# More weight units converted during attention, tail work queued behind the evacuations, and two operands of x kept in float32

## The chip, the cores and the metric

The kernel runs on one core of a Trainium2 chip. The metric is the device time of one execution in microseconds, as the median of several. TensorE (PE in the profile) multiplies matrices into PSUM banks, VectorE (DVE), ScalarE (ACT) and GpSimd (POOL) work elementwise, and SyncE (SP) issues the DMAs. Each engine runs its own instructions in the order in which the program holds them.

## The reference

Attention with normalised queries and keys, and then two feed-forward blocks. The weights of both blocks come in float64.

```python
q_n, k_n = rmsnorm(q, g_q), rmsnorm(k, g_k)                # (4, 12, 448, 64)
attn = softmax(q_n @ k_n.T / 8)
x = (attn @ v).transpose(0, 2, 1, 3).reshape(1792, 768)
x = ((x @ w1) * (x @ w2) @ w3) @ w_out                     # 768 -> 1024 -> 1024 -> 768
h = x @ w_in                                               # 768 -> 2048
out = (h * clip(h + 3, 0, 6) / 6) @ w_out2                 # 2048 -> 768
```

## The kernel before, in words

Every float32 operand of a large product is split into a high and a low part (`t[:, 0]` by ACT, `t[:, 1]` as the difference, by DVE or POOL: `halves`), and a product is three matmuls. A float64 weight is turned into float32 on the chip by `convert`: two ACT instructions (L142, L143) and two DVE instructions (L145, L148).

The attention of 48 head pairs runs in steps of 112 x 448 scores (`attention`). In each step `fill` lets a filler go on: `products`, which makes w3 @ w_out first and then, batch by batch, `layer1` (x @ w1 and x @ w2, evacuated from PSUM by L366, L369 and L371) and `layer2` (with the folded w3 @ w_out, evacuated by L411 and stored to `x2d`). Their operand tiles `ws` are loaded again for each batch, three units ahead. `fill` also lets `early` go on, which converts weight units of the last block ahead of time, half a unit at a time: load into `raw`, convert, store as float32 to `wfd`. A unit is 128 x 768; `units2` lists the 32 units (16 of w_in, 16 of w_out2) in their order of use, and the last `NE` are converted in `early`. The others are `fresh`: they are loaded into `wr` and converted whole, into `wf`, by `units` and `spend`.

After the attention a loop (L1052 and on; the tail from here) runs the rest of `products`: the end of layer2 of the third batch, then layer1 and layer2 of the last one. Beside it go the fresh units and, from the end of the last layer1 on, the preparation of x for the first pair of batches (`xprep`), and of the first weights (`prep_to`).

The last block runs for two pairs of batches, p = 0 and 1. x @ w_in is made by a Strassen scheme with seven products (`ORDER`, P1 to P7) of nine matmuls each on 384-wide halves. Two PSUM banks, sA and sB, take them in turn: a product that adds to a bank, or starts it anew, waits until the bank's earlier content was copied (`L1123 u<-sA`, `u<-sB`) or added (L1131). The operands of x are 11, 21, T1, T2, T3 (from `xprep`), 22 and T4 (from `xrest`, which loads 22 again and makes T4 as the difference of the split parts of 21 and T2, by L976 to L978). Behind the Strassen products of p = 0 stands the M stage: 324 matmuls (items "M", layer4) on the second batch, whose operands `g` are split by `gsplit` (L1085, L1086), and beside which x of p = 1 is prepared by `xprep` and `xrest`.

A scheduler fixes the order on each engine when the program is built; `tc.issue_after(i)` makes what is written in its block stand behind instruction i on i's engine, and adds no wait for it.

Of the kernel before, what the change touches and what calls it, by code (L numbers as in the profile page):

```python
# [27 lines left out]
P = 128  # L28
# [17 lines left out]
NE = 18  # L46
# [5 lines left out]
def fused_kernel(ctx: ExitStack, tc: tile.TileContext, nat, qT, kT, vin, gq, gk,  # L52
# [103 lines left out]
    def products():  # L156
        yield from wprime()
        for b in range(B):
            yield from layer1(b)
            if b == 0:  # L160
                L["early"] = early()
            if b == B - 1:
                for _ in L["early"]:
                    pass
                L["xm"].__exit__(None, None, None)
                L["half"] = True
            yield from layer2(b)
# [136 lines left out]
    L = {}  # L304
# [3 lines left out]
    def open_l1():  # L308
# [14 lines left out]
        def item(u):  # L323
# [19 lines left out]
            else:  # L343
                src = w12d[r // 2, 1 - r % 2] if r < 2 * M1 else wpd[r - 2 * M1].rearrange("p k c -> p (k c)")
                dma(t.bitcast(F32).rearrange("p t c -> p (t c)"), src)
# [16 lines left out]
    def layer1(b):  # L362
        pool = L["pool"]

        def evac_b(ps, bs):
            nc.scalar.activation(bs, ps[:, :S], AF.Copy)  # L366

        def evac_a(m, ps, bs):
            nc.vector.tensor_mul(bs, ps[:, :S], bs)  # L369
            d = pool.tile([P, 2, S], F32R, tag="abh", bufs=M1, name="abh")  # L370
            nc.scalar.activation(d[:, 0, :], bs, AF.Copy)  # L371
            nc.vector.tensor_sub(d[:, 1, :], bs, d[:, 0, :])
            L["abh"][m] = d
# [32 lines left out]
    def layer2(b):  # L406
        pool = L["pool"]

        def evac(n, ps):
            st = pool.tile([P, S], F32, tag="bs", bufs=2, name="bs")  # L410
            nc.scalar.activation(st, ps[:, :S], AF.Copy)  # L411
            L["last"] = dma(x2d[b, n], st)

        for n in range(KD):
            ps = bank("f")
            for a in range(M1):
# [19 lines left out]
    def fill(us, aux):  # L436
# [7 lines left out]
        state["early"] = min(state["early"] + 0.7, 1.4)  # L444
# [435 lines left out]
    def units():  # L880
        n = 0
        for v, (kind, q) in enumerate(uses):
# [3 lines left out]
            if v in fresh:  # L886
                r = wr.pop(v)
# [5 lines left out]
                n += 1  # L893
                load_raw(n + 1)
# [52 lines left out]
    def xprep(p):  # L947

        b1, b2 = PAIRS[p]
        for k in range(KD // 2):  # L950
            x = {}
            for z, b, n in (("11", b1, k), ("21", b1, k + 3), ("12", b2, k), ("22", b2, k + 3)):
                x[z] = utile()
                dma(x[z], x2d[b, n])
# [3 lines left out]
            for z, src in (("11", x["11"]), ("21", x["21"]), ("T2", t2), ("T1", t1)):  # L958
                xo[z, k] = halves(xtile(z, k), src)
                yield 1.2  # L960
            nc.vector.tensor_sub(x["12"], x["22"], x["12"])
# [3 lines left out]
    def xrest(p):  # L965
        x = []
        for k in range(KD // 2):
            x.append(utile())
            dma(x[k], x2d[PAIRS[p][1], k + 3])
        yield 0.0  # L970
        for k in range(KD // 2):
            xo["22", k] = halves(xtile("22", k), x[k])
            yield 1.2
        for k in range(KD // 2):
            d = utile()
            nc.vector.tensor_sub(d, xo["21", k][:, 0, :], xo["T2", k][:, 0, :])  # L976
            nc.vector.tensor_sub(x[k], xo["21", k][:, 1, :], xo["T2", k][:, 1, :])
            nc.vector.tensor_add(d, d, x[k])  # L978
            xo["T4", k] = halves(xtile("T4", k), d)
            yield 1.8  # L980
# [62 lines left out]
    load_raw(1)  # L1043
# [8 lines left out]
    while not state["done"] or any(k >= now[0] for k in tasks):  # L1052
# [3 lines left out]
        if now[0] % 2 and "half" not in L:  # L1056
            spend(1.5)
        if "half" in L:
            if xg is None:
                xo["cm"] = tc.tile_pool(name="xl", bufs=1, side="left", **RW)  # L1060
                xo["pool", True] = d1.enter_context(xo["cm"])
                xg = xprep(0)
            for _ in range(2):
                if next(xg, None) is None:
                    prep_to(ready[0] + 1 if ready[0] < AHEAD2 else 0)
# [15 lines left out]
    G, g = {}, {}  # L1081

    def gsplit(p, b, q, src):
        t = rp.tile([P, 2, S], F32R, tag="g", bufs=4, name="g")
        nc.scalar.activation(t[:, 0, :], src, AF.Copy)  # L1085
        nc.vector.tensor_sub(t[:, 1, :], src, t[:, 0, :])  # L1086
# [73 lines left out]
    next(xg)  # L1160
    for i, it in enumerate(items):
# [6 lines left out]
        next(xg, None)  # L1168
# [58 lines left out]
```

## Time and profile before

| | us |
|---|---|
| median of the runs (3) | 1203.75 |
| lowest, highest | 1199.5, 1210.93 |
| the profiled execution | 1209.22 |
| its span, first to last instruction | 1207.4 |
| TensorE busy in it | 1144.1 (95%) |

TensorE's end times are modelled, so that 25 us of work without a gap show as 25 us busy; the number of its instructions in a stretch tells more. A row of a timeline has the start and the duration, and in brackets how long the engine sat idle before, and on what.

### The profile page before, as it was taken

The numbers are of one execution on the slowest core, as the hardware profiler recorded it, in microseconds if no ns is written. First come the engines' busy times: TensorE is split into PE (matmuls) and PEld (weight loads), VectorE is DVE, ScalarE is ACT, GpSimd is POOL, SyncE is SP. The second block draws the span as 40 slices with busy tenths as digits, with TensorE's granted clock in tenths as the row PEclk, the third lists the DMA queues.
The fourth block names the chain that finished last, engine by engine and source line by source line (L and its number), as shares of the span: only waits on it lengthen the run. The fifth ranks groups of instructions, "written<-read, shape, count | busy, mean of one in ns | idle before, by whom it ended". The sixth has DMA issues, their size and how long they took to land.

```text
span 1207.4 us, 17322 instructions
## 1 busy us (share of the span) xinstructions
PE 1144.1 (95%) x5596; PEld 977.9 (81%) x5596; DVE 844.8 (70%) x1775; ACT 762.0 (63%) x1589; POOL 352.7 (29%) x297
## 2 busy tenths in 40 slices
PE   3689899999999999999998999899999799999998
PEld 1345577788789998889998999699999699999997
DVE  6969887899788889887765456655547765555542
ACT  5869877888787787777754355455556455555542
POOL 1123312555333124222022013322224832223221
PEclk9799999899899999999999999899999999999999
DMA  8888755488999888887689887422236242222301
GB/s 270 281 288 288 255 156 161 156 265 267 330 338 316 286 289 295 283 284 256 226 302 405 319 305 284 162 89 66 84 90 226 89 150 80 71 87 74 125 31 46
DMA packets 88890, 252.71 MB, mean 209 GB/s; under 512 B 11232, under 2 KB 35040, under 8 KB 88800
## 3 DMA queue, kind: packets, MB, share of 16 engines
q1 hardware_dynamic: 88800, 251.61, 62.5%
q8 instruction: 44, 0.72, 0.2%
q14 instruction: 46, 0.38, 0.1%
HBM read 208.93 MB, written 42.64 MB: 208 GB/s over the span
## 4 chain that ended last, share of the span: by engine, by line
PE 74%; DVE 9%; DMA 7%; issue 4%; ACT 3%; POOL 2%; SPq 1%; ACTq 0%; DVEq 0%; POOLq 0%
PE bank L390 12%; PE sB L1111 8%; PE sA L1111 8%; PE bank L395 6%; PE acc L86 5%; PE acc L87 5%; PE acc L88 5%; PE bank L645 4%; PE bank L251 3%; PE bank L86 3%; PE bank L87 2%; PE bank L88 2%; PE bank L619 2%; PE bank L620 2%; PE bank L698 2%
## 5 line engine op out<-in xcount | busy, mean ns | idle before, releaser
L390 PE MATMUL bank<-xhl,ws 128*128 128x448 f32 x768 | 181.9, 370 | 3.3 <-ACT bs L366 3.1
L944 POOL TENSOR_TENSOR wt<-wf,wt 128x384 fp32r<-128x384 f32 x90 | 105.2, 1172 | 216.5 <-ACT wt L942 210.9
L390 PEld LDWEIGHTS bank<-xhl,ws 128*128 128x128 f32 x768 | 145.1, 190 | 17.3 <-ACT bs L366 3.4
L638 ACT ACTIVATE PP<-PP,mx 112x448 f32<-112x448 f32 x192 | 127.2, 663 | 41.1 <-DVE mx L633 39.1
L626 DVE CUSTOM_DVE_ANT_0 PP<-bank,rb,rq 112x448 f32<-112x448 f32 x192 | 128.7, 675 | 24.4 <-PE bank L620 14.7
L87 PE MATMUL acc<-g,wt 128*128 128x448 f32 x384 | 141.6, 369 | 3.5 <-DVE g L1086 3.5
L88 PE MATMUL acc<-g,wt 128*128 128x448 f32 x384 | 136.7, 370 | 4.7 <-POOL wt L944 3.5
L86 PE MATMUL acc<-g,wt 128*128 128x448 f32 x384 | 127.8, 369 | 0.0
L942 ACT ACTIVATE wt<-wf 128x384 fp32r<-128x384 f32 x176 | 89.8, 519 | 59.9 <-PE acc L88 36.1
L1111 PE MATMUL sA<-xo,wt 128*128 128x448 f32 x504 | 113.8, 368 | 3.4 <-ACT xo L942 2.5
L1111 PE MATMUL sB<-xo,wt 128*128 128x448 f32 x504 | 114.2, 371 | 1.3 <-ACT u L1123 1.2
L251 PE MATMUL bank<-woh,w 128*128 128x384 f32 x256 | 100.2, 518 | 10.9 <-DVE wst L244 7.2
L654 ACT ACTIVATE xh<-bank 128x448 fp32r<-128x448 f32 (+1 forms) x156 | 82.9, 539 | 35.8 <-PE bank L645 33.2
L1111 PEld LDWEIGHTS sA<-xo,wt 128*128 128x128 f32 x504 | 95.0, 189 | 12.8 <-ACT xo L942 3.3
L1111 PEld LDWEIGHTS sB<-xo,wt 128*128 128x128 f32 x504 | 95.7, 190 | 10.5 <-ACT u L1123 1.5
L645 PEld LDWEIGHTS bank<-ident,PP 112*128 112x128 f32 x672 | 79.2, 142 | 28.8 <-issue 10.8
L619 PE MATMUL bank<-K,Q 128*112 128x448 f32 x192 | 81.2, 424 | 21.6 <-ACT K L598 11.2
L645 PE MATMUL bank<-ident,PP 112*128 112x112 f32 x672 | 94.4, 262 | 3.7 <-DVE xl L664 3.1
L395 PE MATMUL bank<-xhl,ws 128*128 128x448 f32 x384 | 96.0, 368 | 0.0
L664 DVE TENSOR_TENSOR xl<-bank,xh 128x448 fp32r<-128x448 f32 x142 | 87.0, 616 | 8.7 <-ACT xh L654 7.6
L944 DVE TENSOR_TENSOR wt<-wf,wt 128x384 fp32r<-128x384 f32 x86 | 53.5, 623 | 52.1 <-ACT wt L942 49.3
L145 DVE SCALAR_TENSOR_TENSOR raw<-raw 128x384 int32<-128x384 int32 (+1 forms) x100 | 66.5, 667 | 28.8 <-ACT raw L143 27.8
(131 smaller groups left out, 2429.8 us busy)
## 6 DMA issues: line engine op xcount, KB each, us to landing
ws<-w12d SPq DMA_DIRECT2D x48, 768.0 KB
wf<-wfd SPq DMA_DIRECT2D x82, 384.0 KB
ws<-wpd SPq DMA_DIRECT2D x32, 768.0 KB
raw<-in_wo_dram SPq DMA_DIRECT2D x36, 384.0 KB
raw<-in_w_dram SPq DMA_DIRECT2D x32, 384.0 KB
w12d<-ws SPq DMA_DIRECT2D x16, 768.0 KB
qr<-in_qT_dram SPq DMA_DIRECT2D x24, 448.0 KB
kr<-in_kT_dram SPq DMA_DIRECT2D x24, 448.0 KB
```

Source lines behind the costliest of these rows:

```text
L86: nc.tensor.matmul(ps, lh, rh, start=first, stop=False)
L87: nc.tensor.matmul(ps, lh, rl, start=False, stop=False)
L88: return nc.tensor.matmul(ps, ll, rh, start=False, stop=last)
L251: nc.tensor.matmul(ps[:, :NH], W["w3"][a, c // 4][:, cs], W["woh"][c, n], start=c == 0, stop=c == M1 - 1)
L390: nc.tensor.matmul(ps[:, :S], w[:, 0, ks], x[:, y, :], start=k == 0 and y == 0, stop=False)
L395: nc.tensor.matmul(ps[:, :S], w[:, 1, ks], L["xhl"][i][:, 0, :], start=False, stop=k == KD - 1)
L619: nc.tensor.matmul(ps[:CP, :S], qs, k1[:, j, :], start=True, stop=False)
L626: anchors[8 * i + s].append(nc.vector.tensor_tensor_reduce(out=T["PP", i][:, c, sl], in0=ps[:CP, :S], in1=T["rb", i][:, sl], op0=ALU.mult, ...
L638: anchors[8 * i + s].append(nc.scalar.activation(v, v, AF.Exp, bias=T["m", i][:, 8 + s : 9 + s], accum_out=T["sum", i][:, s : s + 1]))
L645: nc.tensor.transpose(ps[:, c * CP : c * CP + CP], src[:, c, kb * P : kb * P + P], ident[:CP, :CP])
L944: (nc.vector if nsplit[0] % 2 else nc.gpsimd).tensor_sub(t[:, 1, :], src, t[:, 0, :])
L1111: mm = nc.tensor.matmul(ps[:, :S], w[:, a, ks], x[:, c, :], start=first and k == 0 and n == 0, stop=k == KD // 2 - 1 and n == 2, skip_grou ...
```

## The change

`NE` goes from 18 to 24, and `early` gets a budget of 0.95 (at most 1.9) for each step, before 0.7 (1.4); it begins with the second block of layer2 of the first batch. Eight units are then left for the tail. There, `spend`, `xprep` and `prep_to` are written in a block that queues what they issue behind the last evacuation on ACT and on DVE and behind the last load of `ws` on SP (`L["gate"]`). `xprep` puts 22 into a tile of float32 (with the tag of `wr`) and T4 = 21 - T2 into another, with one subtraction each; `xrest` only splits them. In the M stage the preparation of x advances in three of four items, behind the last `gsplit`. The diff, cut to its core:

```diff
 NF = 5
-NE = 18
+NE = 24
...
-                dma(t.bitcast(F32).rearrange("p t c -> p (t c)"), src)
+                L["gate"]["sp"] = dma(t.bitcast(F32).rearrange("p t c -> p (t c)"), src)
                 yield 0.0
...
         def evac_b(ps, bs):
-            nc.scalar.activation(bs, ps[:, :S], AF.Copy)
+            L["gate"]["act"] = nc.scalar.activation(bs, ps[:, :S], AF.Copy)
...
-            nc.vector.tensor_sub(d[:, 1, :], bs, d[:, 0, :])
+            L["gate"]["dve"] = nc.vector.tensor_sub(d[:, 1, :], bs, d[:, 0, :])
...
         def evac(n, ps):
             st = pool.tile([P, S], F32, tag="bs", bufs=2, name="bs")
-            nc.scalar.activation(st, ps[:, :S], AF.Copy)
+            L["gate"]["act"] = nc.scalar.activation(st, ps[:, :S], AF.Copy)
             L["last"] = dma(x2d[b, n], st)
 
         for n in range(KD):
             ps = bank("f")
+            if b == 0 and n == 1:
+                L["early"] = early()
...
             state["aux"] -= c
-        state["early"] = min(state["early"] + 0.7, 1.4)
...
             if v in fresh:
+                n += 1
+                load_raw(n)
                 r = wr.pop(v)
                 if r.dtype == F32:
                     nc.gpsimd.tensor_copy(t, r)
                     yield 0.9
                 else:
                     yield from convert(t.bitcast(I32), r)
-                n += 1
-                load_raw(n + 1)
...
         b1, b2 = PAIRS[p]
+        for z in ("22", "T4"):
+            t = mp.tile([P, DM, 2], I32, tag="wr", bufs=2, name="wr").rearrange("p n t -> p (n t)")
+            xo[z] = t.bitcast(F32)[:, : KD // 2 * S].rearrange("p (k s) -> p k s", s=S)
         for k in range(KD // 2):
-            x = {}
+            x = {"22": xo["22"][:, k]}
             for z, b, n in (("11", b1, k), ("21", b1, k + 3), ("12", b2, k), ("22", b2, k + 3)):
-                x[z] = utile()
+                if z != "22":
+                    x[z] = utile()
                 dma(x[z], x2d[b, n])
             t1, t2 = utile(), utile()
...
             for z, src in (("11", x["11"]), ("21", x["21"]), ("T2", t2), ("T1", t1)):
                 xo[z, k] = halves(xtile(z, k), src)
                 yield 1.2
+            nc.vector.tensor_sub(xo["T4"][:, k], x["21"], t2)
+            yield 0.6
             nc.vector.tensor_sub(x["12"], x["22"], x["12"])
             xo["T3", k] = halves(xtile("T3", k), x["12"])
             yield 1.8
 
     def xrest(p):
-        x = []
-        for k in range(KD // 2):
-            x.append(utile())
-            dma(x[k], x2d[PAIRS[p][1], k + 3])
-        yield 0.0
-        for k in range(KD // 2):
-            xo["22", k] = halves(xtile("22", k), x[k])
-            yield 1.2
-        for k in range(KD // 2):
-            d = utile()
-            nc.vector.tensor_sub(d, xo["21", k][:, 0, :], xo["T2", k][:, 0, :])
-            nc.vector.tensor_sub(x[k], xo["21", k][:, 1, :], xo["T2", k][:, 1, :])
-            nc.vector.tensor_add(d, d, x[k])
-            xo["T4", k] = halves(xtile("T4", k), d)
-            yield 1.8
+        for z in ("22", "T4"):
+            for k in range(KD // 2):
+                xo[z, k] = halves(xtile(z, k), xo[z][:, k])
+                yield 1.2
...
         fill(2.0, 3.0)
         run_tasks()
-        if now[0] % 2 and "half" not in L:
-            spend(1.5)
-        if "half" in L:
+        if "half" in L and xg is None:
+            xo["cm"] = tc.tile_pool(name="xl", bufs=1, side="left", **RW)
+            xo["pool", True] = d1.enter_context(xo["cm"])
+            xg = xprep(0)
+        with ExitStack() as es:
+            for z in L["gate"].values():
+                es.enter_context(tc.issue_after(z.ins))
             if xg is None:
-                xo["cm"] = tc.tile_pool(name="xl", bufs=1, side="left", **RW)
-                xo["pool", True] = d1.enter_context(xo["cm"])
-                xg = xprep(0)
-            for _ in range(2):
-                if next(xg, None) is None:
-                    prep_to(ready[0] + 1 if ready[0] < AHEAD2 else 0)
+                spend(1.1)
+            else:
+                for _ in range(2):
+                    if next(xg, None) is None:
+                        prep_to(ready[0] + 1 if ready[0] < AHEAD2 else 0)
...
         t = rp.tile([P, 2, S], F32R, tag="g", bufs=4, name="g")
-        nc.scalar.activation(t[:, 0, :], src, AF.Copy)
-        nc.vector.tensor_sub(t[:, 1, :], src, t[:, 0, :])
+        done[:] = [nc.scalar.activation(t[:, 0, :], src, AF.Copy), nc.vector.tensor_sub(t[:, 1, :], src, t[:, 0, :])]
         g[p, b, q] = t
...
     for i, it in enumerate(items):
...
         prep_to(i + AHEAD2)
         kind, p, q = it[:3]
-        next(xg, None)
+        with ExitStack() as es:
+            if kind == "M":
+                for z in done:
+                    es.enter_context(tc.issue_after(z.ins))
+            if kind != "M" or q % 2 == 0 or it[4] == 0:
+                next(xg, None)
```

What follows is word for word the order of instructions at three places. Lines of the changed kernel are two to four lower there (L409 is L411 of before, L364 is L366, L1119 is L1123, L1074 is L1077, L1082 is L1085 or L1086).

ACT, at the start of the last layer1 (`wr` is a fresh unit being converted, `wt<-wf` and `wt<-sx` splits of the first Strassen weights, `bs` an evacuation), before:

```order
L142 ACTIVATE wr<-wr 128x768
L143 ACTIVATE wr<-wr 128x768
L411 ACTIVATE bs<-bank 128x448
L942 ACTIVATE wt<-wf 128x384 x2
L411 ACTIVATE bs<-bank 128x448
L942 ACTIVATE wt<-sx 128x384 x4
L942 ACTIVATE wt<-wf 128x384
L142 ACTIVATE wr<-wr 128x768
L143 ACTIVATE wr<-wr 128x768
L366 ACTIVATE bs<-bank 128x448
```

Now:

```order
L142 ACTIVATE wr<-wr 128x768
L143 ACTIVATE wr<-wr 128x768
L409 ACTIVATE bs<-bank 128x448
L142 ACTIVATE wr<-wr 128x768
L143 ACTIVATE wr<-wr 128x768
L364 ACTIVATE bs<-bank 128x448
L369 ACTIVATE abh<-bs 128x448
L364 ACTIVATE bs<-bank 128x448
L369 ACTIVATE abh<-bs 128x448
L142 ACTIVATE wr<-wr 128x768
```

The splits of the Strassen weights are gone from here, and the evacuations of layer1 stand behind two conversions.

ACT, at the first Strassen products of p = 0, from the copy of P1 (`u<-sA`) over that of P6 (the second `u<-sA`) to that of P5 (`u<-sB`), before:

```order
L1123 ACTIVATE u<-sA 128x448
L942 ACTIVATE wt<-wf 128x384
L411 ACTIVATE bs<-bank 128x448
L942 ACTIVATE wt<-sx 128x384
L1077 ACTIVATE u<-u,half 128x448
L411 ACTIVATE bs<-bank 128x448
L1123 ACTIVATE u<-sA 128x448
L942 ACTIVATE wt<-wf 128x384
L942 ACTIVATE xo<-u 128x448 x2
L1085 ACTIVATE g<-u 128x448
L942 ACTIVATE xo<-u 128x448
L1123 ACTIVATE u<-sB 128x448
```

Now:

```order
L1119 ACTIVATE u<-sA 128x448
L942 ACTIVATE wt<-wf 128x384
L942 ACTIVATE wt<-sx 128x384
L942 ACTIVATE xo<-wr 128x448 x2
L1074 ACTIVATE u<-u,half 128x448
L942 ACTIVATE xo<-wr 128x448 x4
L1119 ACTIVATE u<-sA 128x448
L942 ACTIVATE wt<-wf 128x384
L1082 ACTIVATE g<-u 128x448
L1119 ACTIVATE u<-sB 128x448
```

The six splits of 22 and T4 (`xo<-wr`) stand ahead of the copies of P6 and P5; before, one evacuation and one weight split stood between L1077 and the copy of P6.

DVE, in the M stage of p = 0 (`xo<-u` splits of x, `u<-xo` and the `u<-u` of L978 the making of T4, `g<-G` the low part of g), before:

```order
L976 TENSOR_TENSOR u<-xo 128x448 x2
L944 TENSOR_TENSOR xo<-u,xo 128x448
L976 TENSOR_TENSOR u<-xo 128x448
L1086 TENSOR_TENSOR g<-G,g 128x448
L944 TENSOR_TENSOR xo<-u,xo 128x448
L977 TENSOR_TENSOR u<-xo 128x448
L1086 TENSOR_TENSOR g<-G,g 128x448
L978 TENSOR_TENSOR u<-u 128x448
L977 TENSOR_TENSOR u<-xo 128x448
L944 TENSOR_TENSOR wt<-wf,wt 128x384
L978 TENSOR_TENSOR u<-u 128x448
```

Now (L965 makes T4, L960, L961 and L967 the other sums of x):

```order
L1082 TENSOR_TENSOR g<-G,g 128x448
L961 TENSOR_TENSOR u<-wr,u 128x448
L944 TENSOR_TENSOR wt<-wf,wt 128x384 x2
L965 TENSOR_TENSOR wr<-u 128x448
L1082 TENSOR_TENSOR g<-G,g 128x448
L967 TENSOR_TENSOR u<-wr,u 128x448
L944 TENSOR_TENSOR wt<-wf,wt 128x384
L1082 TENSOR_TENSOR g<-G,g 128x448
L960 TENSOR_TENSOR u<-u 128x448
```

The nine instructions that make T4 are three, and splits of weights stand between the sums of x.

## Rows read from the trace of the kernel before

**Rows 1.** From the view of windows of 25 us: us, busy us (instructions) of each engine, PEclk, DMA share, GB/s.
```profile
650.00:675.00 25.00, 21.93 (x101) 19.65 (x101) 14.79 (x23) 10.75 (x18) 2.30 (x2) 0.93 0.99 388
750.00:775.00 25.00, 19.07 (x77) 15.39 (x76) 19.98 (x26) 10.30 (x21) 12.81 (x10) 0.86 0.67 249
775.00:800.00 25.00, 25.00 (x124) 23.00 (x123) 12.26 (x22) 13.27 (x27) 6.36 (x7) 1.00 0.21 64
925.00:950.00 25.00, 21.49 (x98) 19.19 (x97) 19.77 (x32) 11.36 (x24) 19.68 (x9) 0.93 0.42 129
950.00:975.00 25.00, 21.36 (x103) 18.90 (x102) 19.16 (x22) 12.71 (x27) 13.86 (x11) 1.00 0.42 139
```

**Rows 2.** From the timeline of ACT, 650 to 662 us: start, us, instruction, idle before and releaser.
```profile
656.16 0.52 ACT L942 ACTIVATE wt<-sx 128x384 fp32r<-128x384 f32 x1 [2.00 <-DVE sx L1022]
...
657.01 0.88 ACT L142 ACTIVATE wr<-wr 128x768 f32<-128x768 f32 x1
...
658.56 0.52 ACT L366 ACTIVATE bs<-bank 128x448 f32<-128x448 f32 x1
```

**Rows 3.** From the timeline of PE, 650 to 662 us.
```profile
659.13 3.19 PE L390 MATMUL bank<-xhl,ws 128*128 128x448 f32 x8 [3.07 <-ACT bs L366]
```

**Rows 4.** From the chain of waits, 625 to 662 us: start, us, what.
```profile
638.09 7.12 DMA wr<-in_win_dram
```

**Rows 5.** From the timeline of PE, 740 to 775 us.
```profile
769.89 2.12 PE L1111 MATMUL sB<-xo,wt 128*128 128x448 f32 x9 [1.16 <-ACT u L1123]
```

**Rows 6.** From the DVE groups, 744 to 766 us: count, busy us, mean ns, idle before.
```profile
L148 DVE SCALAR_TENSOR_TENSOR wf<-wr 128x768 int32<-128x768 int32 x2 | 3.7, 1842 | 0.0
L977 DVE TENSOR_TENSOR u<-xo 128x448 f32<-128x448 f32 x3 | 2.8, 936 | 0.0
L978 DVE TENSOR_TENSOR u<-u 128x448 f32<-128x448 f32 x3 | 2.6, 880 | 0.0
L976 DVE TENSOR_TENSOR u<-xo 128x448 f32<-128x448 f32 x3 | 1.8, 616 | 0.0
```

**Rows 7.** From the timeline of ACT, 740 to 775 us.
```profile
748.59 1.04 ACT L942 ACTIVATE xo<-u 128x448 fp32r<-128x448 f32 x2
...
756.91 0.67 ACT L1077 ACTIVATE u<-u,half 128x448 f32<-128x448 f32 x1 [5.00 <-DVE u L1131]
```

**Rows 8.** From the timeline of DVE, 740 to 775 us.
```profile
753.07 1.58 DVE L977 TENSOR_TENSOR u<-xo 128x448 f32<-128x448 f32 x1
```

**Rows 9.** From the timeline of POOL, 740 to 775 us.
```profile
749.24 4.93 POOL L944 TENSOR_TENSOR xo<-u,xo 128x448 fp32r<-128x448 f32 x3 [10.59 <-ACT xo L942]
```

**Rows 10.** From the timeline of PE, 936 to 966 us.
```profile
945.67 0.74 PE L88 MATMUL acc<-g,wt 128*128 128x448 f32 x1 [3.51 <-POOL wt L944]
...
964.12 0.47 PE L87 MATMUL acc<-g,wt 128*128 128x448 f32 x1 [3.55 <-DVE g L1086]
```

**Rows 11.** From the timeline of POOL, 903 to 982 us.
```profile
918.68 1.02 POOL L944 TENSOR_TENSOR wt<-wf,wt 128x384 fp32r<-128x384 f32 x1 [2.99 <-ACT wt L942]
...
934.30 15.17 POOL L944 TENSOR_TENSOR wt<-wf,wt 128x384 fp32r<-128x384 f32 x5 [3.20 <-ACT wt L942]
```

**Rows 12.** From the timeline of DVE, 903 to 982 us.
```profile
953.32 1.42 DVE L977 TENSOR_TENSOR u<-xo 128x448 f32<-128x448 f32 x1 [8.55 <-POOL xo L944]
```

**Rows 13.** From the view of windows, the attention stage and one stretch in it.
```profile
310.00:632.00 322.00, 318.17 (x1734) 284.38 (x1733) 262.40 (x650) 239.06 (x524) 82.78 (x67) 0.99 0.87 290
320.00:330.00 10.00, 8.66 (x33) 7.68 (x34) 5.64 (x17) 4.46 (x12) 2.31 (x2) 0.66 0.89 316
```

**Rows 14.** From the groups by line and form, 310 to 632 us: count, busy us, mean ns, idle before.
```profile
L148 DVE SCALAR_TENSOR_TENSOR raw<-raw 128x384 int32<-128x384 int32 x38 | 24.7, 650 | 0.4
...
L143 ACT ACTIVATE raw<-raw 128x384 int32<-128x384 uint16 x38 | 20.7, 544 | 0.0
```

**Rows 15.** From the waits, 310 to 632 us: who waited for whom, us, times, longest us.
```profile
ACT raw L142 <- DMA raw<-in_wo_dram: 10.1, 6, 3.2
...
PE bank L86 <- DMA ws<-wpd: 1.9, 1, 1.9
```

More of the change, by code (lines that the diff above doesn't have):

```diff
@@ L159, in products @@
             yield from layer1(b)
-            if b == 0:
-                L["early"] = early()
             if b == B - 1:
@@ L302, in early @@
             yield 0.0
-    L = {}
+    L = dict(gate={})
     NU = 2 * M1 + 8
@@ L443, in fill @@
             state["aux"] -= c
-        state["early"] = min(state["early"] + 0.7, 1.4)
+        state["early"] = min(state["early"] + 0.95, 1.9)
         while state["early"] > 0 and "early" in L:
@@ L1042, in fused_kernel @@
     load_raw(0)
-    load_raw(1)
     ready = [0]
@@ L1079, in nonlinear @@
                                               op0=ALU.min, op1=ALU.mult), u
-    G, g = {}, {}
+    G, g, done = {}, {}, []
     def gsplit(p, b, q, src):
         t = rp.tile([P, 2, S], F32R, tag="g", bufs=4, name="g")
-        nc.scalar.activation(t[:, 0, :], src, AF.Copy)
-        nc.vector.tensor_sub(t[:, 1, :], src, t[:, 0, :])
+        done[:] = [nc.scalar.activation(t[:, 0, :], src, AF.Copy), nc.vector.tensor_sub(t[:, 1, :], src, t[:, 0, :])]
         g[p, b, q] = t
@@ L1159, in fused_kernel @@
     xg = xrest(0)
-    next(xg)
     for i, it in enumerate(items):
```

## The prediction

> **What bounds the kernel now.** TensorE is the bound: the table has it busy for 95% of the span, and its instructions are the same before and after. A change can only fill or open gaps on it, so I looked for these first, in windows of 25 us. In a window without a gap of the last block PE starts 124 matmuls of 128 x 448, one every 25 / 124 = 0.2016 us [rows 1]. Three places fall short. At 650 to 675 us there are 101, 23 too few, or 4.6 us; at 750 to 775 us 77, 47 too few, 9.5 us; at 925 to 975 us 98 and 103, together 47 too few, 9.5 us. That is 23.6 us in all, what the change can win at most at these places. These figures hold the clock too: where PEclk shows 0.86 or 0.93, part of the window ran at the lower of the two levels after a gap.
>
> Then I asked each place what PE waits for.
>
> *First place, 655.9 to 659.1 us.* PE waits 3.07 us for the evacuation L366 of a bank [rows 3]. The evacuation is ready early, but stands on ACT behind the splits of Strassen weights, which wait for DVE (2.00 us), and behind a conversion of a fresh unit of some 0.9 us an instruction [rows 2]. Those weights are first needed behind the last layer2.
>
> *Second place, the start of the Strassen products.* ACT sits idle 5.00 us for DVE (L1131) [rows 7], and PE 1.16 us for the copy of a Strassen product (L1123) [rows 5]. DVE is the bound there: it makes T4 with nine instructions and ends two conversions, 3.7 + 2.8 + 2.6 + 1.8 = 10.9 us in a stretch of 22 us [rows 6], and part of it runs beside POOL's splits of x (4.93 us for three [rows 9]).
>
> *Third place, the M stage of p = 0.* PE waits 3.51 us for a weight split on POOL and 3.55 us for a low part of g on DVE [rows 10]. Five weight splits on POOL take 15.17 us where one takes 1.02 us [rows 11], since DVE is dense with the preparation of x; then DVE waits 8.55 us for POOL [rows 12].
>
> **The change, part by part.**
>
> *The tail's order (first place).* In the new order the Strassen splits are gone from there, and between the two evacuations in question ACT has one or two conversions, of two instructions of 0.88 us each [rows 2]. A fresh unit's load landed after 7.12 us in this crowded stretch [rows 4]. The two loads are now issued about one evacuation ahead of the first conversion, one product of 24 matmuls, 4.8 us. A bank is needed again one product of layer1 after it was filled, 18 x 0.2016 = 3.6 us; a conversion of 1.8 us and an evacuation of 0.52 us fit in that with 1.3 us to spare. If the load comes 7.12 - 4.8 = 2.3 us late, 1.0 us stays. If it lands only after 10 us, as one beside many others might, 2.6 us stay. I take 0.3 us, nearest to the loads seen. **Gain 4.3 us** (2.0 to 4.6).
>
> *T4 and 22 (second place).* Of the 10.9 us on DVE all go: T4 is made by three subtractions that now stand ahead of the products, and no conversion is left there. But the six splits of 22 and T4 are now one run, on ACT ahead of the copies of P6 and P5. From the end of P1 ACT has its copy, two weight splits and six splits of x, nine copies at 1.04 / 2 = 0.52 us each, and L1077 at 0.67 us, 5.35 us by [rows 7], and then the copy of P6, to 5.9 us. P7, which adds to the same bank, could start after P2's last two matmuls, P6 and P5, 20 x 0.2016 = 4.0 us. So 1.9 us stay at the least. The low parts of these six splits are a run on POOL as well, at 4.93 / 3 = 1.64 us each [rows 9]; while it lasts, an instruction of DVE with two inputs takes 1.58 us [rows 8] instead of 0.62, the mean of L976 without POOL [rows 6]. Some four of them stand on the path from P2 over L1131 and L1078 to the copy of P5: 4 x 0.96 = 3.8 us, of which half may lie beside ACT's run. With 1.9 + 1.9 us and some 1.2 us at the lower clock, 5.0 us stay. **Gain 4.5 us** (0 to 7.6).
>
> *The M stage (third place).* DVE's load between 920 and 970 us falls by the nine T4 instructions and rises by three; that and the spacing of the preparation over 24 of 32 items, behind g, takes the dense run away that starved POOL. Loads of 22 no longer wait for a free buffer behind POOL, as they stand in the tile of the `wr` tag. At 1.02 us [rows 11] five weight splits on POOL take 5 us instead of 15, and items have their weights six items ahead, so that PE should hardly wait. What is left is the start of the stage, where the new order still holds g, weight splits and sums of x close together; I leave a quarter of the loss, 2.5 us. **Gain 7.0 us** (3.5 to 9).
>
> *Six more units in attention.* Twelve halves, each with two DVE instructions of 0.65 us (L145 taken as L148) and two on ACT of 0.54 us [rows 14]: 15.6 us of DVE and 13.0 us of ACT. From 310 to 632 us DVE is idle for 322 - 262.4 = 59.6 us and ACT for 83 us [rows 13], so there is room. The 38 conversions already in that stretch go beside a PE that has 3.8 us of gaps in all [rows 13], at most 0.1 us for each. ACT waited 10.1 us for the raw loads and PE hardly [rows 15]. The added traffic, 12 x (384 + 192) KB or 7.1 MB, is 22 GB/s over the stretch; at 290 GB/s and a share of 0.87 [rows 13] the DMA engines go to about 0.94. So the cost lies between -2 us (the one wait for `ws`, 1.9 us [rows 15], might move) and the whole DVE time, 15.6 us. I take 2.5 us, near the bound by the 38. **Cost 2.5 us.** Six units that are loaded as float32 later instead of converted lie beside a queue at a share of 0.21 [rows 1], at nothing; they cost something only where a load comes late, and they are needed tens of us later.
>
> **The sum.** 4.3 + 4.5 + 7.0 - 2.5 = 13.3 us. From the profiled execution, 1209.2 us, that gives 1195.9 us; that execution is 5.5 us above the median of the runs, in parts of the program that the change leaves alone as far as I can see. From the median, 1203.75 us, it gives **1190.5 us**, 1.1% less.
>
> **The rivals.**
>
> *The run of splits keeps the second stall.* If ACT's and POOL's runs delay P7, P3 and P4 by as much as T4 did, only 4.3 + 7.0 - 2.5 = 8.8 us are won: 1195 us. For it: three splits on POOL took 4.93 us [rows 9], six would take 9.9 us, and between the end of P1 and P3 the new order has 32 matmuls, 6.5 us. Against it: T4's parts are needed two products and some matmuls later than 22's. [...]
>
> *The M stage still stalls.* If the loads of x or DVE's order there still hold g back, 4.3 + 4.5 - 2.5 = 6.3 us are won: 1197.5 us. For it: the sums of x still wait for loads that SP issues behind the outputs of the first batch, and g stands behind them on DVE.
>
> *Attention pays in full.* If DVE's added 15.6 us come out on PE, the gains of 15.8 us are gone: 1203.5 us. Against it stand 59.6 us of idle time.
>
> *Slower: loads of `ws` come late.* SP issues in order, and a raw load or a store of a converted half that waits for DVE holds the loads of `ws` behind it; with a third more halves there are more such waits. Once, PE waited 1.9 us for `ws<-wpd`, and the clock stood at 0.66 in the 10 us after [rows 13, 15], which costs about 3.4 us more: 5.3 us a time. Three times cancel the gains, five give 1203.75 + 26.5 - 15.8 = 1214.5 us. For it: a share of 0.94. Against it: units of `ws` are loaded three ahead, and with 38 conversions it came once.
>
> **How the numbers follow.** The forecast has 55%, the run of splits 17%, the M stage 12%, attention in full 10%, late loads 6%. The forecast's own terms spread from about 1184 to 1196 us. To leave out no more than 2 in 10 the range goes to 1181 us, where the second place gives its upper bound, and to 1202 us, which takes in the first two rivals and most of the third. About 1% is what a measurement of this kernel can tell from no change, and 1% below the median is 1191.7 us, just above the forecast: 0.48 faster by more than that, 0.45 within, 0.07 slower.
>
> **What would show it.** In the profile of the changed kernel: at the start of the last layer1 no wait of PE for L366 of more than 1 us; at the first Strassen products no `u<-xo` on DVE, PE waiting for the copies of P6 and P5 on ACT, and some 100 matmuls in the worst 25 us instead of 77; in the M stage POOL's weight splits at 1 to 1.4 us and over 115 matmuls in each 25 us; from 310 to 632 us gaps on PE of 4 to 7 us. I would be wrong if PE waited for `ws` from DMA several times in attention, if ACT's conversions in the tail waited for loads ahead of an evacuation, or if the run on POOL held P3 and P4.

## The result and the profile after

The changed kernel takes **1188.61 us** (median of 6 runs, 1184.26 to 1193.02) against 1204.16 us, a ratio of 0.9866 with a 95% interval of 0.9826 to 0.9906: 15.6 us less. 1190.5 us were forecast. Its profiled execution has a span of 1186.6 us.

The view of windows of the changed kernel, at the places of [rows 1] and [rows 13], with its columns:

```profile
310.00:632.00 322.00, 316.36 (x1727) 282.56 (x1726) 272.35 (x668) 244.69 (x540) 79.14 (x65) 0.99 0.91 306
...
650.00:675.00 25.00, 24.27 (x120) 22.18 (x119) 11.34 (x14) 10.30 (x15) 0.00 (x0) 1.00 1.00 392
725.00:750.00 25.00, 23.88 (x116) 21.23 (x115) 24.83 (x28) 15.68 (x34) 16.70 (x13) 1.00 0.51 181
750.00:775.00 25.00, 24.59 (x120) 22.25 (x119) 18.38 (x29) 12.41 (x24) 8.66 (x8) 1.00 0.50 174
925.00:950.00 25.00, 25.00 (x123) 22.74 (x122) 22.23 (x25) 13.45 (x31) 20.57 (x14) 1.00 0.37 111
950.00:975.00 25.00, 25.00 (x124) 22.90 (x123) 19.38 (x29) 13.86 (x29) 11.09 (x10) 1.00 0.46 149
```

Where PE started 101 matmuls in 25 us it now starts 120; where it started 77, 116 and 120; in the M stage 123 and 124, without a gap. The granted clock stands at 1.00 in all these windows. In [rows 1] it stood at 0.93, 0.86 and 0.93 of 25 us each. At these three places of the kernel before, windows of 1 us have it at 1.00 or at 0.50, and between the two only where it changes; from 946.21 to 948.45 us, at 0.50, PE starts a matmul every 0.37 us, and from 948.78 to 949.80 us, back at 1.00, every 0.20 us. Taken in proportion, the three figures are worth 1.75 + 3.5 + 1.75 = 7.0 us of work: some 7 of the 23.6 us that the prediction counted were, by this estimate, the lower level around the waits, and went with the waits. What is left at the first Strassen products are short waits, by the view of waits of the changed kernel, 740 to 775 us (who waited for whom, us in total, times, longest us):

```profile
PE sA L1107 <- ACT u L1119: 1.1, 2, 0.7
PE sA L1107 <- DVE u L1075: 0.4, 1, 0.4
```

The first line is for the copies of P1 (0.41 us) and P6 (0.71 us); the copy of P6 stands behind the run of splits of 22 and T4. The timeline of ACT shows both copies and that run, and that of POOL its low parts:

```profile
740.89 0.54 ACT L1119 ACTIVATE u<-sA 128x448 f32<-128x448 f32 x1
...
742.15 1.05 ACT L942 ACTIVATE xo<-wr 128x448 fp32r<-128x448 f32 x2
743.15 0.67 ACT L1074 ACTIVATE u<-u,half 128x448 f32<-128x448 f32 x1
743.73 1.97 ACT L942 ACTIVATE xo<-wr 128x448 fp32r<-128x448 f32 x4
745.60 0.52 ACT L1119 ACTIVATE u<-sA 128x448 f32<-128x448 f32 x1
```

```profile
742.80 8.43 POOL L944 TENSOR_TENSOR xo<-wr,xo 128x448 fp32r<-128x448 f32 x6 [1.84 <-DMA x2d<-bs]
```

**How stretches are compared.** All kernels here have 5596 matmuls, in one order up to no. 1294 (from 0) and behind no. 3666, and with small differences of order between. The program is cut at the matmuls that start in the first profile of the kernel before at 300, 632, 740, 780, 920 and 1000 us (nos. 1138, 2922, 3426, 3575, 4259 and 4604), and the length of a stretch is the difference of their start times in the one profiled execution of each kernel (the first stretch begins with the first matmul). This gives, in us:

| kernel | median | ratio to before (95%) | start to 300 | attention | tail | first products | M stage |
|---|---|---|---|---|---|---|---|
| before | 1204.16 | 1 | 288.9 | 332.0 | 107.9 | 40.1 | 79.9 |
| before, second profile | one run, 1201.32 | | 285.3 | 329.0 | 107.3 | 40.2 | 79.5 |
| changed | 1188.61 | 0.9866 (0.9826 to 0.9906) | 287.6 | 333.2 | 103.2 | 32.9 | 71.1 |
| low parts of 22, T4 on DVE | 1188.98 | 0.9872 (0.9843 to 0.9902) | 285.9 | 335.5 | 103.1 | 32.2 | 71.1 |
| no queueing in the tail | 1190.07 | 0.9883 (0.9851 to 0.9915) | 286.6 | 335.5 | 104.2 | 31.8 | 71.1 |
| M stage behind g, every item | 1189.64 | 0.9868 (0.9845 to 0.9890) | 289.5 | 333.3 | 102.2 | 32.9 | 72.7 |
| M stage three of four, not behind g | 1193.38 | 0.9904 (0.9882 to 0.9926) | 290.4 | 331.1 | 102.3 | 32.9 | 75.9 |
| M stage neither | 1196.67 | 0.9925 (0.9895 to 0.9956) | 286.4 | 336.3 | 105.0 | 32.8 | 76.4 |
| old T4 and 22 | 1197.42 | 0.9939 (0.9917 to 0.9962) | 287.3 | 336.4 | 104.2 | 41.0 | 72.2 |
| 21 units | 1193.73 | 0.9917 (0.9890 to 0.9945) | 284.1 | 329.2 | 103.9 | 39.9 | 71.1 |
| 18 units | 1198.33 | 0.9951 (0.9930 to 0.9972) | 286.9 | 331.4 | 102.8 | 45.8 | 71.1 |
| 18 units, no queueing | 1199.31 | 0.9961 (0.9941 to 0.9981) | 283.8 | 333.8 | 103.1 | 42.7 | 71.1 |
| 18 units, no queueing, old T4 and 22 | 1196.44 | 0.9931 (0.9907 to 0.9955) | 291.2 | 331.3 | 104.3 | 39.8 | 72.5 |
| 32 units | 1210.46 | 1.0061 (1.0034 to 1.0088) | 289.7 | 345.2 | 117.0 | 31.4 | 71.1 |

From 780 to 920 us all have 140.1 us, and from 1000 us on 203.4 us. The first 300 us, in which the kernels are alike, spread from 283.8 to 291.2 us between executions: a stretch says more of a part than the whole time does. Not every stretch is equally steady. The five kernels with 24 units, the block in the tail and the new T4 are alike in attention and tail, and yet spread from 331.1 to 336.3 us in the one and from 102.2 to 105.0 in the other; the four of them that are alike at the first products have 32.8 to 32.9 us there. The kernels below the changed one were measured in three later series; the kernel before had medians of 1206.38, 1205.09 and 1205.53 us in these, so times from different series compare by their ratios.

### The profile page after: what moved, and what is told of

It reads as the page before. It is cut to its first block, busy times and chain, and to the rows that moved or that the text cites. A ratio compares the mean times of both kernels' runs of the same rounds, so it can differ in the third digit from the quotient of the medians.

```text
span 1186.6 us, 17363 instructions
## 1 busy us (share of the span) xinstructions
PE 1133.6 (96%) x5596; PEld 971.4 (82%) x5596; DVE 849.3 (72%) x1775; ACT 760.3 (64%) x1601; POOL 346.5 (29%) x297
## 5 line engine op out<-in xcount | busy, mean ns | idle before, releaser
L944 POOL TENSOR_TENSOR wt<-wf,wt 128x384 fp32r<-128x384 f32 x84 | 93.6, 1117 | 208.7 <-ACT wt L942 203.1
L1107 PE MATMUL sB<-xo,wt 128*128 128x448 f32 x504 | 112.4, 366 | 0.0
L944 DVE TENSOR_TENSOR wt<-wf,wt 128x384 fp32r<-128x384 f32 x92 | 63.1, 688 | 59.3 <-ACT wt L942 59.1
L619 PE MATMUL bank<-K,Q 128*112 128x448 f32 x192 | 80.2, 419 | 24.5 <-DVE mx L626 13.3
L145 DVE SCALAR_TENSOR_TENSOR raw<-raw 128x384 int32<-128x384 int32 (+1 forms) x112 | 69.9, 626 | 43.6 <-ACT raw L143 41.6
```

The lines of the kernel that those rows point to most:

```text
L944: (nc.vector if nsplit[0] % 2 else nc.gpsimd).tensor_sub(t[:, 1, :], src, t[:, 0, :])
L1107: mm = nc.tensor.matmul(ps[:, :S], w[:, a, ks], x[:, c, :], start=first and k == 0 and n == 0, stop=k == KD // 2 - 1 and n == 2, skip_grou ...
```

## The experiments

**The kernel before, profiled again.**

> The kernel before, profiled once more, since its first profiled execution lay 5 us above the median. Theory: the wait for ws near 319 us and the half clock behind it, 3 to 5 us, were that excess; here PE has no wait of over 1 us from 310 to 335 us, and the places at 650, 750 and 925 to 975 us stall as before. Rival: the wait is in every execution of this order of early, and the excess was spread; then it stands here too.

Its span is 1199.5 us, 7.9 us less than in the first profile. The view of windows of this second profile, 320 to 330 us, beside the second line of [rows 13]:

```profile
320.00:330.00 10.00, 10.00 (x55) 9.14 (x54) 8.06 (x21) 8.15 (x20) 4.02 (x5) 1.00 1.03 334
```

55 matmuls instead of 33, and PE waits nowhere for `ws`. So the wait of 1.9 us and the lower clock behind it (0.66 in the first profile, 1.00 here) do not stand in every execution, as the theory had it: attention has 329.0 instead of 332.0 us, and 3.6 us more lie in the first 300 us. The three places lose as much as in the first profile. But in the M stage the waits divide otherwise: in the first profile 3.51 us were for a weight split on POOL and 3.55 for g, here, by the view of waits of PE, 912 to 992 us:

```profile
PE acc L87 <- DVE g L1086: 5.1, 3, 3.6
PE acc L88 <- POOL wt L944: 0.7, 1, 0.7
```

**T4 and 22 (second place).** "old T4 and 22" puts the old `xprep` and `xrest` into the changed kernel:

```diff
-            nc.vector.tensor_sub(xo["T4"][:, k], x["21"], t2)
...
+            nc.vector.tensor_sub(d, xo["21", k][:, 0, :], xo["T2", k][:, 0, :])
+            nc.vector.tensor_sub(x[k], xo["21", k][:, 1, :], xo["T2", k][:, 1, :])
+            nc.vector.tensor_add(d, d, x[k])
```

> The changed kernel, but with 22 loaded again and T4 made from the split parts by nine instructions of DVE, as before. The changed kernel is at 1188.6 us. Theory: these nine, and their wait for POOL's low parts, made the second place and at least the half of the third; 7.2 us come back at the first Strassen products and 4 to 9 in the M stage, 1200 to 1205 us. Rival: the order of the tail and the spacing in the M stage took the stalls away by themselves; then it stays within 3 us, 1186 to 1192 us.

1197.42 us, between the two. The first products are at 41.0 us, so the whole gain of 7.2 us there hangs on T4 and 22. The M stage, against the theory, stays at 72.2 us, where the changed kernel has 71.1. At the first products the timeline of PE has the old stall in a new form:

```profile
756.67 0.74 PE L87 MATMUL acc<-g,wt 128*128 128x448 f32 x1 [2.98 <-DVE g L1087]
```

L1087 is the low part of g; on DVE it stands behind three L977 and two L976, which make T4.

The other edit makes the low parts of the six splits on DVE:

```diff
-                xo[z, k] = halves(xtile(z, k), xo[z][:, k])
+                xo[z, k] = halves(xtile(z, k), xo[z][:, k], nc.vector)
```

> The changed kernel with the six low parts of 22 and T4 made by DVE instead of POOL, at 0.61 us each. Theory: POOL's run of 8.4 us slows DVE's instructions beside it from 0.6 to 1.5 us, eight of them, 7 us, against 3.7 us of added work; what is left of the second place, 2.9 us from 725 to 775 us, falls by 1 to 2 us: 1186.5 to 1188 us. Rival: DVE is the bound there, and six more instructions ahead of the copies of P6 and P5 cost PE 2 to 4 us: 1190.5 to 1193 us.

1188.98 us, no difference in the whole time; the first products have 32.2 us instead of 32.9. Its timeline of DVE:

```profile
744.18 1.15 DVE L944 TENSOR_TENSOR xo<-wr,xo 128x448 fp32r<-128x448 f32 x2
745.25 0.61 DVE L1075 SCALAR_TENSOR_TENSOR u<-u 128x448 f32<-128x448 f32 x1
```

And that of the changed kernel:

```profile
745.73 1.56 DVE L1075 SCALAR_TENSOR_TENSOR u<-u 128x448 f32<-128x448 f32 x1
```

There L1075 takes 1.56 us beside POOL, without POOL 0.61 us. The run on POOL does slow DVE here, but to take it away, with six instructions of 0.55 to 0.61 us added on DVE, gives PE 0.7 us, less than the theory said.

**The order of the tail (first place).**

```diff
-            for z in L["gate"].values():
-                es.enter_context(tc.issue_after(z.ins))
```

> The changed kernel without the block that queues the tail's conversions and preparation behind the evacuations and loads. Theory: the wait of PE for an evacuation at the start of the last layer1 is back, some 3 us and the clock behind it, 1193 us, and little changes elsewhere. Rival: with six units fewer in the tail the weights come late enough or early enough by themselves; no wait of PE over 1 us from 632 to 700 us, 1187 to 1190 us.

1190.07 us, at the upper end of the rival. The tail has 104.2 us, against 107.3 to 107.9 before, and lies within the 102.2 to 105.0 us of the kernels with the block: no gain of the block is shown. PE waits once, 1.58 us, for the evacuation, and this does not stand behind the splits but waits itself for a store, by the timeline of ACT:

```profile
658.58 0.54 ACT L364 ACTIVATE bs<-bank 128x448 f32<-128x448 f32 x1 [2.52 <-DMA x2d<-bs]
```

So the gain is there without the block, and as the next kernels show, without the six units as well.

**How many units go to attention.** `NE` and the budget alone ("18 units"), then 18 units without the block ("18 units, no queueing"), then that with the old T4 and 22 as well, and 21 units (budget 0.82, at most 1.65):

```diff
-NE = 24
+NE = 18
...
-        state["early"] = min(state["early"] + 0.95, 1.9)
+        state["early"] = min(state["early"] + 0.7, 1.4)
```

> The changed kernel with 18 units converted in attention at the old budget, so that 14 are left for the tail. Theory: the six units cost 1 to 2.5 us in attention, which are won, and six conversions more in the tail, queued behind the evacuations, cost 0 to 5 us there; 1186 to 1193 us, and first and second place stay without the old stalls. Rival: the six units fewer in the tail made the gain at the first and second place; both stalls come back, 1188.6 + 11.9 - 1.2 = 1199 us.

> 18 units in attention and no queueing behind the evacuations: of the change only 22 and T4 in float32, the spacing in the M stage and the later raw loads are left. Theory: the queueing is what pushed the conversions of the kernel with 18 units into the first Strassen products, and it needs the six units fewer; without both, the wait of PE of 3 us for an evacuation at the start of the last layer1 is back, and nothing at the first products: 1188.6 + 4.7 - 1.7 = 1191.6 us, 1189 to 1194. Rival: 14 units are too many for the tail in any order; 10 us or more come back from 632 to 780 us, 1197 to 1203 us.

> 18 units in attention, no queueing, and 22 and T4 made as before: of the change only the spacing in the M stage, the pace of the conversions in the tail and the later raw loads are left. Theory: the stall of 7.3 us at the first products with 18 units (1199.3 us) comes from the tiles of 22 and T4, which stand in the buffers of the fresh units and wait for the last conversion; without them no wait of PE over 3 us for a copy from 725 to 750 us, the old loss of 9.5 us behind it instead, 1194 to 1198 us. Rival: the slower pace of conversions makes the stall, it stays and the old one is added: 1204 to 1208 us.

> The changed kernel with 21 units converted in attention (budget 0.82, at most 1.65), so that 11 are left for the tail. Theory: the stall at the first products is a threshold, reached only where the last conversion falls behind the loads of 22; three units more in the tail still fit, and attention gives back about 1 us: 1186 to 1189 us. Rival: it grows with each unit, 12 to 14 us for six, so some 6 us for three: 1192.5 to 1196 us.

1198.33, 1199.31, 1196.44 and 1193.73 us. The tail is at 102.8 to 104.3 us in all, so the stall at the first place does not come back. The loss is at the first products: 45.8 us with 18 units, 42.7 without the block, 39.9 with 21, where the changed kernel has 32.9. The rivals had the sizes right in the first two and in the last (though in the first not the cause, since the first place stays free), the theory in the third. "18 units, no queueing" shows how, in its timelines of PE, ACT and DVE:

```profile
747.40 2.98 PE L1105 MATMUL sA<-xo,wt 128*128 128x448 f32 x7 [7.26 <-ACT u L1117]
```

```profile
746.80 0.55 ACT L1117 ACTIVATE u<-sA 128x448 f32<-128x448 f32 x1 [3.82 <-DVE wr L965]
```

```profile
743.37 1.88 DVE L148 SCALAR_TENSOR_TENSOR wf<-wr 128x768 int32<-128x768 int32 x1
745.28 1.97 DVE L965 TENSOR_TENSOR wr<-u 128x448 f32<-128x448 f32 x2
```

The copy of P1 waits for L965, which makes T4 into a buffer of the `wr` tag; L965 stands behind the last conversion of a fresh unit (L148), which reads a `wr` buffer. With the old T4 and 22 in the same kernel (39.8 us) that wait is gone and the old stall is back. With 21 units no conversion is left there; the preparation of x, behind three conversions more, ends late itself (its last L965 112.4 us behind the start of the tail, in the changed kernel 107.9 us), ACT holds the copy behind the six splits that need it, and PE waits 4.83 us. So the float32 T4 pays only where the conversions end early: it is worth 8.1 us with 24 units (41.0 to 32.9) and costs 2.9 us with 18 and no queueing (39.8 to 42.7).

**More units.** All 32 units ahead of time:

```diff
-NE = 24
+NE = 32
...
-        state["early"] = min(state["early"] + 0.95, 1.9)
+        state["early"] = min(state["early"] + 1.27, 2.54)
```

> The changed kernel with all 32 units converted in attention (budget 1.27, at most 2.54, a step), none in the tail. Theory: the cost by unit stays small, 1.7 us for six, so 2 to 5 us more for eight, and the tail has nothing left to win over 1 to 2 us; 1189 to 1193 us. Rival: the DMA queues, at a share of 0.91 with 24 units, are full, loads of ws come late and the clock falls behind them; three or more waits of PE for ws from 310 to 632 us, over 1196 us.

1210.46 us, slower than before: attention 345.2 us, tail 117.0 us. The conversions do not end with the attention: the last L148 of `early` starts 54 us into the tail (in the changed kernel 16 us). PE does not wait for `ws` from a DMA, so the rival had the size and not the cause. In attention its waits are many and short, for DVE and ACT (the longest 2.1 us). In the tail 8.16 us are one wait of PE for an evacuation (L364), and the chain of waits of this kernel shows it (start, us, what):

```profile
657.93 8.52 DMA x2d<-bs
...
666.46 8.19 DMA wf<-wfd
...
674.71 7.38 DMA x2d<-bs
...
682.20 0.55 ACT bs L364
```

ACT has two tiles `bs`; it waits 12.84 us until the stores of the last ones to `x2d` have landed, beside the loads of converted units (`wf<-wfd`), 96 in this kernel and 88 in the changed one. From 632 to 690 us the DMA engines are at a share of 0.99.

**The M stage (third place).** Three edits of one place: neither spacing nor the place behind g (its edit is shown); three of four items, but not behind g; every item, but behind g.

```diff
         with ExitStack() as es:
-            if kind == "M":
-                for z in done:
-                    es.enter_context(tc.issue_after(z.ins))
-            if kind != "M" or q % 2 == 0 or it[4] == 0:
-                next(xg, None)
+            next(xg, None)
```

> The changed kernel with the preparation of x advanced in every item of the M stage and not queued behind the splits of g. Theory: the stalls in the M stage hung on T4 made from split parts, behind which g stood on DVE; without the spacing 0 to 4 us come back there, 1188.6 to 1193 us. Rival: the dense run on DVE that starves POOL is made by the pace, not by T4; the 9 us of the third place come back, 1197.5 us.

> The changed kernel with the preparation of x in three of four items of the M stage, but not queued behind the splits of g. Theory: it is the place behind g that counts, since the M stage lost nothing with DVE busier than before; 3 us or more of the 8 us that the kernel without the spacing loses stay, with PE waiting for g on DVE: 1192 to 1197 us. Rival: the thinner pace does it alone: 1188 to 1190 us and no wait of PE over 1 us from 920 to 975 us.

> The changed kernel with the preparation of x advanced in every item of the M stage, but queued behind the splits of g. Theory: as the place behind g is what counts, PE does not wait there for over 1 us and the time is that of the changed kernel, 1187 to 1190.5 us. Rival: the denser pace starves POOL or delays g: 3 to 8 us come back, 1192 to 1197 us.

1196.67, 1193.38 and 1189.64 us: the first is near the rival, the others are as the theory had it. In the M stage they have 76.4, 75.9 and 72.7 us, where the changed kernel has 71.1. The place behind g is worth 3.7 us, both together 5.3 us; the pace alone gives 0.5 us, about what the two profiles of before differ by there. Without both, PE waits for g, by the timeline of PE of that kernel:

```profile
933.17 0.48 PE L87 MATMUL acc<-g,wt 128*128 128x448 f32 x1 [1.44 <-DVE g L1082]
...
939.85 0.74 PE L87 MATMUL acc<-g,wt 128*128 128x448 f32 x1 [2.80 <-DVE g L1082]
```

So the rival had the size and not the cause. The groups of POOL's weight splits in this stage (count, then shortest, middle and longest ns), first without both, then in the changed kernel:

```profile
L944 POOL TENSOR_TENSOR wt<-wf,wt x10: 1012/1324/1400, 915.2 to 960.1; 128x384 fp32r<-128x384 f32 x10
L944 POOL TENSOR_TENSOR wt<-wf,wt x10: 1022/1398/5929, 912.4 to 952.8; 128x384 fp32r<-128x384 f32 x10
```

Without both no split on POOL is held up, and PE waits 4.2 us for g; in the changed kernel one split is held up for 5.93 us, and PE does not wait. With the thinner pace alone PE waits 1.98 us for g and twice, 1.2 us together, for splits on POOL.

Without spacing and place the stage has 76.4 us, against 79.7 before (the mean of the two profiles); of what differs, T4 in float32 is the likely cause of these 3.3 us, but it was not tried alone. Beside the new place the old T4 costs 1.1 us (72.2 to 71.1), and 0.87 us of that are one wait behind the M stage, at the first Strassen products of p = 1.

## Why the prediction was right, and where its reasons were not

**The net** was sized at 13.3 us; the medians differ by 15.6 us. The first profile's excess over the median was of that execution, as the sum had assumed: of the 7.9 us to the second profile 3.0 lie in attention, where the wait for `ws` stood, and 3.6 in the first 300 us, ahead of the change. The three gains were forecast at 15.8 us together and come to 19.7 to 20.8 us by the stretches.

**First place, gain 4.3 us.** 4.1 to 4.7 us, the right size, by luck: the reason given, the new order behind the evacuations, is not shown to carry any of it. "18 units, no queueing, old T4 and 22" has neither that block nor the six units nor the new T4, and is at 104.3 us. In it three of the Strassen splits still stand ahead of the evacuation and wait 2.10 us for DVE, by its timeline of ACT:

```profile
657.64 1.35 ACT L942 ACTIVATE wt<-sx 128x384 fp32r<-128x384 f32 x3 [2.10 <-DVE sx L1022]
658.90 0.53 ACT L364 ACTIVATE bs<-bank 128x448 f32<-128x448 f32 x1
```

What is missing against [rows 2] are the fourth split, with its own wait of 2.00 us, a split of `wf`, and the conversion of a fresh unit, two instructions of 0.88 us. The slower, even pace of `spend` and the raw loads one at a time are what this kernel has left of the change in the tail; which of the two did it was not tried apart, and the cause of this gain stays open. In the changed kernel one of the prediction's own signs of being wrong did come, a conversion that waits for its load ahead of an evacuation (timelines of ACT and PE):

```profile
650.96 0.91 ACT L142 ACTIVATE wr<-wr 128x768 f32<-128x768 f32 x1 [3.30 <-DMA wr<-in_win_dram]
...
652.54 0.53 ACT L409 ACTIVATE bs<-bank 128x448 f32<-128x448 f32 x1
```

```profile
653.13 1.08 PE L388 MATMUL bank<-xhl,ws 128*128 128x448 f32 x4 [0.73 <-ACT bs L409]
```

It cost 0.73 us, between the 0.3 us that were taken and the 1.0 us that the sum's own working gives for a load of 7.12 us. By the same working a load of 10 us leaves 10 - 4.8 - 1.3 = 3.9 us, not 2.6, so the lower bound of this gain should have been 0.7 us and not 2.0.

**Second place, gain 4.5 us.** The mechanism held, the term was too small: 7.2 us. The 5.0 us that were to stay are 1.5 us (32.9 against 31.4, the shortest of any kernel). The copy of P6 started 4.7 us behind that of P1 (745.60 against 740.89) where 5.35 were reckoned, PE waited 0.7 us instead of 1.9, and no lower clock followed (1.00 from 725 to 775 us). POOL's run took 8.43 us, not 9.9, and moving it to DVE gave 0.7 us where the sum had 1.9 for it: the instructions that it slows mostly lie beside work of PE. The first rival, that the run keeps the stall, falls with this.

**Third place, gain 7.0 us.** 8.4 to 8.8 us; here the step failed, not the size. The prediction took DVE's density, which was to starve POOL, for the cause, and expected the dense run to be gone and POOL's weight splits at 1 to 1.4 us. It read "five weight splits take 15.17 us" as five slow ones; by the timeline of POOL they were one that was held up and four quick ones, and the changed kernel's run of six (12.74 us) is of the same kind. Before, then now:

```profile
934.30 11.32 POOL L944 TENSOR_TENSOR wt<-wf,wt 128x384 fp32r<-128x384 f32 x1 [3.20 <-ACT wt L942]
945.58 3.88 POOL L944 TENSOR_TENSOR wt<-wf,wt 128x384 fp32r<-128x384 f32 x4
```

```profile
924.23 5.93 POOL L944 TENSOR_TENSOR wt<-wf,wt 128x384 fp32r<-128x384 f32 x1 [3.00 <-ACT wt L942]
930.13 6.84 POOL L944 TENSOR_TENSOR wt<-wf,wt 128x384 fp32r<-128x384 f32 x5
```

DVE is busier now than before (22.23 + 19.38 = 41.6 of 50 us, against 38.9 before; over 50 us from the start of the stage in each, 46.5 against 40.7), and in the kernel with the old T4 busier still, with no gap on PE, by the view of windows of that kernel:

```profile
925.00:975.00 50.00, 50.00 (x244) 45.52 (x243) 46.85 (x56) 25.98 (x57) 33.81 (x23) 1.00 0.44 141
```

Being held up on POOL was part of the loss in the first profile, 3.51 us of waits, but only 0.7 us in the second, with the same loss. What counts most is the order: g, which PE needs at once, stands ahead of the sums of x, which are needed tens of us later. The quarter of the loss that was left for g, weight splits and sums standing close together did not arise.

**Attention, cost 2.5 us.** Against the two profiles of before the changed kernel has 1.2 and 4.2 us more. Over all profiles, the seven with 24 units have a mean of 334.5 us (331.1 to 336.4), the five with 18 units 331.5 (329.0 to 333.8): 3.0 us for six units, give or take 2.5 by the spread of the profiles. The bound that the prediction named, 0.1 us a half, gives 1.2 us for the twelve; the 2.5 that it took are twice that, and nearer. The third rival (15.6 us) and the fourth (late `ws`) did not come about; PE's waits from 310 to 632 us are for scores and evacuations, 5.6 us of gaps in all, where 4 to 7 were named.

**What was not priced** is that the parts need each other. The sum gave the six units a cost alone. They are also what makes room for T4 and 22: without them the first products lose 12.9 us (45.8 against 32.9). As the forecast was made for all parts together, its number stood.

Two small readings of the prediction are off. PE's wait at the first place runs from 656.06 to 659.13 us, not from 655.9. And a window also counts a matmul that began ahead of it. In the M stage of the changed kernel PE starts a matmul every 0.207 us by its timeline, not every 0.2016, which changes the sums by 2 to 3%.

## What to carry to other kernels

Undo the parts of a change in pairs too: here one part gives a buffer and time away, and another makes them free, so that each alone won nothing and together they win. Where an engine is dense and its reader stalls, look first at what stands ahead of the needed instruction in the queue, and put the work that is due later behind it; in the M stage thinning the work did little (0.5 us), moving it did most (3.7 us). A queue that hides six more units at 0.5 us each need not hide eight more: part of the cost came back in another place, at stores of 8.52 and 7.38 us, with the DMA engines at a share of 0.99.

## What the runs showed of the hardware

*A split on POOL was held up for ten of DVE's instructions and more in two places, and not in another.* In the changed kernel POOL's run of six weight splits goes from 924.23 to 936.97 us; the first takes 5.93 us, the other five 1.40 us each. The timeline of DVE in it:

```profile
928.20 0.61 DVE L967 TENSOR_TENSOR u<-wr,u 128x448 f32<-128x448 f32 x1
928.73 0.55 DVE L944 TENSOR_TENSOR wt<-wf,wt 128x384 fp32r<-128x384 f32 x1
929.46 1.19 DVE L944 TENSOR_TENSOR xo<-u,xo 128x448 fp32r<-128x448 f32 x1 [0.18 <-ACT xo L942]
930.57 1.45 DVE L1082 TENSOR_TENSOR g<-G,g 128x448 fp32r<-128x448 f32 x1
```

Up to 929.28 us DVE's instructions follow each other without a gap and take 0.55 to 0.61 us, and POOL's first split does not end. It ends 0.9 us after the start of DVE's first gap, of 0.18 us, and soon after that gap each of DVE's takes 1.4 us, as long as POOL has splits left. In the kernel before it was the same with the split of 11.32 us: it ended at 945.62 us, 0.9 us after DVE had gone idle at 944.77 us (the wait of [rows 12]). But such a gap did not come first each time. Some 4 us earlier in the changed kernel a split on POOL takes 1.34 us beside two instructions of DVE that follow each other without one (timelines of DVE and POOL):

```profile
919.60 0.61 DVE L1082 TENSOR_TENSOR g<-G,g 128x448 fp32r<-128x448 f32 x1
920.13 1.58 DVE L960 TENSOR_TENSOR u<-u 128x448 f32<-128x448 f32 x1
```

```profile
919.89 1.34 POOL L944 TENSOR_TENSOR xo<-u,xo 128x448 fp32r<-128x448 f32 x1 [1.71 <-ACT xo L942]
```

Why the split on POOL ends only after ten instructions of DVE in one place, and during the second in another, no run here shows.

*A wait of PE was not always followed by the lower clock.* In the changed kernel's attention PE waits 1.26 us at 433.3 us and 1.70 us at 483.8 us. The view of windows:

```profile
430.00:440.00 10.00, 8.44 (x40) 6.61 (x39) 7.27 (x17) 4.77 (x11) 1.47 (x2) 0.83 0.86 333
...
480.00:490.00 10.00, 8.30 (x45) 7.33 (x44) 9.32 (x24) 6.72 (x15) 4.01 (x4) 1.00 0.92 347
```

The shorter wait was followed by a stretch at the lower level, 0.50 in the windows of 1 us from 436 to 439 us; behind the longer one all windows of 1 us up to 495 us have 1.00. The two profiles of the kernel before differ too, 0.66 and 1.00 at 320 to 330 us: the lower clock, with the wait for `ws` ahead of it, stands there in one execution and not in the other.
